# An attention and feed-forward kernel on one core: heads 12 to 15 take the later heads' structure

## The chip, the cores and the metric

The kernel runs on one core of a Trainium2 chip. The metric is the device time of one execution in microseconds, the median of several. The core has TensorE (PE in the profile, with its weight loads as PEld), VectorE (DVE), ScalarE (ACT), GpSimd (POOL) and the queue SP that issues the transfers.

## The reference

Attention over 8 batches of 8 heads, 576 rows and a head dimension of 64, with a mask by blocks of 64 rows, and then a feed-forward layer on the 4608 rows of 512 columns that the heads make together:

```
scores = scale * np.matmul(q, k.transpose(0, 1, 3, 2))
mask = block_i >= block_j                      # blocks of 64
attn = softmax(where(mask, scores, -1e9))      # plus 1e-9 in the sum
x = (attn @ v).transpose(0, 2, 1, 3).reshape(B * S, H * D)
h = x @ w_in                                   # 512 x 2048
out = maximum(0.01 * h, h) @ w_out             # 2048 x 512
```

The weights come as 64-bit floats, and the kernel turns them into pairs of 32-bit parts itself.

## The kernel before

The 64 heads are worked one after the other, two heads making one pair that fills 128 rows of the transposed result. The head's number is `i`, and its batch is `i // 8`. There are two structures of a head, and `PLAIN = 16` (L31) sets where the first ends.

An early head (`i < PLAIN`) loads q and k transposed, scales k (L464), and multiplies in plain 32-bit (L492). The masked rows go through a maximum (L524), an exponential (L533), a reciprocal of the sums (L548, L549) and a scaling (L562 to L564). Then TensorE transposes the probabilities in fifteen blocks (L589), ACT or DVE copies them out of PSUM into `ptf` (L268, L269), and `paired` multiplies them with v for two heads together (L654).

A late head loads q and k in one transfer (`qk_in`, L470), and splits each into a high and a low part in the rounded 32-bit type: `qs` and `ks` (L476 to L483). Its score matmuls run on the parts (L503), its transposes run on VectorE in blocks of 32x32 (`turn`, L677), and four stores to a buffer in device memory and four loads back (`way`, L692, and `ptm`, L699) put the blocks in place. `columns` multiplies with v (L624).

The feed-forward layer runs in 18 chunks of 256 rows. `split_x` splits a chunk's rows into `xh` and `xl` (L739, L740), `ffn1` multiplies with `wih` and `wil` (L755), and `ffn2` with `woh` and `wol` (L782); each chunk has eight steps `u`. A chunk may start once all the heads of its batch are done: chunks 0 and 1 after head 7, chunks 2 and 3 after head 15, and so on. The chunks take turns between `xh0` and `xh1` from chunk 2 on (`side`, L722).

The weights come in 32 pieces (`weight_piece`, L381). A piece is loaded by SP, and built from its integer words on ACT, DVE and POOL (L416 to L440), then split into its two parts. Step `u` of chunk 0 needs the pieces up to number 4u + 4.

The buffers change in three steps. The pools `early` (second row buffers, `ptf`, `vf`, `k_in`, `ident`) and `coded` (the raw words of the weights) are closed when the early heads, and the weights, are done. `second_stage` (L367) puts `qs` and `ks` where `coded` was; `third_stage` (L373) puts `ptm`, `turn`, `vt` and `xh1` where `early` was. A tile in the new pool waits for the tiles whose place it takes.

The order of all instructions is worked out ahead of the launch by `Plan` (L75): a list scheduler with estimated costs, which takes, on each engine, the ready piece of work of the lowest rank. Head `i` has a rank near `i` (first scores `i`, second scores `i + RB`, transposes `i + RT`, values `i + RV`); weight piece n (from 0) has `OFF1 + SL1 * (n + 1) / 32` (L807); step k of the two or three chunks that become ready at head `i` has `i + LEAD + 8k / num` (L833). On the chip every engine works through its list in order.

Of the kernel before, what the change touches and what calls it, by code (L numbers as in the profile page):

```python
# [9 lines left out]
F32 = mybir.dt.float32  # L10
F32R = mybir.dt.float32r
# [6 lines left out]
P = 128  # L18
BLK = 64
D = 64  # L20
S = 576
# [3 lines left out]
CH = 256  # L25
# [2 lines left out]
SIGNS = 5  # L28

WIDE = 512  # L30
PLAIN = 16  # L31
SPREAD = True

RAWS = 3
VALS = 3

RL = -1.611
RP = 20.774
RB = -3.305
RT = 2.986  # L40
RV = -1.976
RX = -2.769
RN = -66.464
RM = -40.088

LEAD = 4.317
LAG = 1.993
RS = -16.364
RG = -5.155
OFF1 = 2.865  # L50
SL1 = 20.541
AHEAD = 0.39

MOVES = {
    "raw": (2200, 675), "k": (900, 1170), "q": (500, 1110), "qk": (1500, 1325), "v": (450, 792),
    "way": (590, 385), "back": (1090, 1095), "out": (690, 354),
}
PADD = 3219.925
HOLD = 72.848
FILL = 235  # L60
FILLTO = -190.328


LOAD = 109
PAD = 463.142
PADO = 31.265
SPARE = 43.439
CHANGE = 100
RATE = 0.449
EDGE = 110  # L70
# [181 lines left out]
def attention_ffn(ctx: ExitStack, tc: tile.TileContext, q2: bass.AP, k2: bass.AP, qk: bass.AP, v: bass.AP, w_in: bass.AP, w_out: bass.AP, out: bass.AP):  # L252
# [3 lines left out]
    ND = DM // P  # L256
# [33 lines left out]
    def fixed(shape, dt, name, n=None, pool=const):  # L290
        if n is None:
            return pool.tile(shape, dt, name=name)
        return [pool.tile(shape, dt, name=f"{name}{i}") for i in range(n)]

    later = {}
# [71 lines left out]
    def second_stage():  # L367
        coded.close()
        pool = ctx.enter_context(tc.tile_pool(name="late", bufs=1, side="right", reuse_waits="tile"))
        later["qs"] = fixed([P, S], F32R, "qs", 2, pool)  # L370
        later["ks"] = fixed([P, 2, S], F32R, "ks", None, pool)

    def third_stage():  # L373
        early.close()
        pool = ctx.enter_context(tc.tile_pool(name="last", bufs=1, reuse_waits="tile"))
        later["ptm"] = fixed([P, turned], F32, "ptm", 2, pool)
        later["turn"] = fixed([P, turned], F32, "turn", 2, pool)
        later["vt"] = fixed([P, NT, D], F32, "vt", 2, pool)
        xh.append(fixed([P, ND, CH], F32R, "xh1", None, pool))

    def weight_piece(num, rank, f, out_side, c0):  # L381
        w, k, kv = WIDE, num % RAWS, num % VALS
# [431 lines left out]
    for i in range(NH + 1):  # L814
        if i == H:
            add([("POOL", 1, narrow)], 0, [], [("h", y) for y in range(2)])
        if i == PLAIN:
            new = [("qs", y) for y in range(2)] + ["kh", "kl"]
            add([("POOL", 1, second_stage)], 0, [y for k in wkeys.values() for y in k], new)
            blocks = ((0, 0), (1, 0), (2, 0), (3, 0), (3, 3), (4, 0), (4, 3), (4, 4))  # L820
            new = [("turn", y, t, j) for y in range(2) for t, j in blocks]
            new += [("ptm", y, b) for y in range(2) for b in range(4)] + [("vt", y) for y in range(2)] + ["qkt"]
            new += [("xh", 1, e) for e in range(0, CH, BLK)]
            old = [("ptf", y, g[0]) for g in tgroups for y in range(2)] + ["ident"]
            old += [(k, y) for k in ("vf", "q", "k") for y in range(2)] + [("p", 1, t) for t in range(1, NT)]
            add([("POOL", 1, third_stage)], 0, [], sorted(set(old), key=str) + new)
        if i in events:
            here = [c for c in range(NCHUNK) if ready[c] == i]
            nxt = events[events.index(i) + 1] if i != events[-1] else i + H
            num = len(here) * NU  # L830
            for k in range(num):
                c, u = here[k // NU], k % NU
                rank = i + LEAD + (nxt - i) * k / num  # L833
                if u == 0:
                    split_x(c, rank - RS)
                ffn1(c, u, rank)
                ffn2(c, u, rank + (nxt - i) * LAG / num + 0.003)
        if i < NH:
            attention(i)
# [37 lines left out]
```

## Time and profile before

| | us |
|---|---|
| median of 3 runs | 1076.86 (1076.47 to 1076.99) |
| the profiled execution | 1080.17 |
| its span, first to last instruction | 1078.4 |
| PE, DVE, ACT, POOL busy | 1053.0, 598.7, 554.3, 237.1 |

The busy times are sums over the whole span. The start, in which weights are built and no chunk is ready, and the end, in which only chunks are left, look different from the middle, so the stretches are read one by one below.

### The profile page before, as it was taken

How to read it: one execution, taken by the hardware profiler on the slowest of the kernel's cores; microseconds unless marked ns; L12 is line 12 of the kernel's file. 1: busy time of each engine (PE TensorE's matmuls, PEld its weight loads, DVE VectorE, ACT ScalarE, POOL GpSimd, SP SyncE). 2: the span in 40 equal slices, each digit the busy share in tenths (PEclk: the TensorE clock that was granted, in tenths of full speed). 3: DMA queues.
4: the chain of work that ended last, by engine and by line, in shares of the span. 5: the costliest groups of instructions: out<-in, count | busy, mean ns of one | idle time of the engine just before them, and what ended most of it. 6: DMA issues, size and time to landing. Idle time of an engine off the chain costs nothing.

```text
span 1078.4 us, 19058 instructions
## 1 busy us (share of the span) xinstructions
PE 1053.0 (98%) x6976; PEld 912.6 (85%) x6976; DVE 598.7 (56%) x1649; ACT 554.3 (51%) x1335; POOL 237.1 (22%) x209
## 2 busy tenths in 40 slices
PE   6889999999999999999999999999999999999998
PEld 4568888988888888888898888898888888999997
DVE  5988882667767677665544567666656660001000
ACT  6998863555545455555544555554555542222222
POOL 3343430221222011112131120212121201221221
PEclk8999999999999999999999999999999999999999
DMA  5555521358777676766454557666676752000000
GB/s 164 167 170 152 171 77 54 111 174 229 219 213 210 187 212 204 197 203 188 140 156 124 172 149 212 194 185 184 181 199 167 212 159 79 2 20 21 1 20 20
DMA packets 89886, 159.07 MB, mean 148 GB/s; under 512 B 9408, under 2 KB 74944, under 8 KB 89792
## 3 DMA queue, kind: packets, MB, share of 16 engines
q1 hardware_dynamic: 89792, 157.85, 50.3%
q8 instruction: 55, 0.90, 0.4%
q14 instruction: 39, 0.32, 0.1%
HBM read 104.33 MB, written 53.48 MB: 146 GB/s over the span
## 4 chain that ended last, share of the span: by engine, by line
PE 86%; DMA 5%; ACT 4%; DVE 3%; issue 1%; SPq 0%; ACTq 0%; DVEq 0%
PE p_h L755 34%; PE p_o L782 33%; PE p_s L503 6%; PE p_t L624 6%; DMA qk_in<-in_qk 3%; PE p_s L492 3%; ACT prow L533 2%; PE p_t L589 1%; PE p_t L654 1%; DVE turn L677 1%; DMA raw<-in_w_out 1%; DVE nmrec L524 1%; DMA raw<-in_w_in 1%; DMA out<-ob 1%; ACT prow L564 0%
## 5 line engine op out<-in xcount | busy, mean ns | idle before, releaser
L755 PE MATMUL p_h<-xh,wih 128*128 128x256 f32 x1152 | 317.7, 281 | 0.4 <-ACT xh L268 0.4
L755 PE MATMUL p_h<-xh,wil 128*128 128x256 f32 x1152 | 314.5, 278 | 0.0
L755 PE MATMUL p_h<-xl,wih 128*128 128x256 f32 x1152 | 299.9, 278 | 0.0
L279 POOL TENSOR_TENSOR gl<-g,gh 128x512 fp32r<-128x512 f32 x115 | 149.5, 1300 | 674.0 <-ACT gh L268 509.5
L755 PEld LDWEIGHTS p_h<-xh,wih 128*128 128x128 f32 x1152 | 216.6, 188 | 12.5 <-issue 2.4
L755 PEld LDWEIGHTS p_h<-xh,wil 128*128 128x128 f32 x1152 | 217.0, 188 | 0.6
L755 PEld LDWEIGHTS p_h<-xl,wih 128*128 128x128 f32 x1152 | 208.1, 188 | 8.2
L533 ACT ACTIVATE prow<-p_s,nmrec 128x448 f32<-128x448 f32 x300 | 154.3, 524 | 91.6 <-DVE nmrec L524 84.6
L770 ACT ACTIVATE g<-p_h 128x512 f32<-128x512 f32 x144 | 85.9, 597 | 221.5 <-PE p_h L755 219.8
L782 PE MATMUL p_o<-woh,gh 128*128 128x512 f32 x576 | 181.2, 396 | 0.0
L782 PE MATMUL p_o<-wol,gh 128*128 128x512 f32 x576 | 179.3, 392 | 0.0
L782 PE MATMUL p_o<-woh,gl 128*128 128x512 f32 x576 | 179.2, 393 | 0.0
L677 DVE STREAM_TRANSPOSE turn<-prow 128x384 f32<-128x384 f32 (+3 forms) x384 | 141.9, 399 | 11.7 <-ACT prow L564 7.8
L782 PEld LDWEIGHTS p_o<-woh,gl 128*128 128x128 f32 x576 | 108.2, 188 | 24.3
L524 DVE TENSOR_REDUCE nmrec<-p_s 128x1 f32<-128x448 f32 x300 | 127.6, 471 | 1.5
L782 PEld LDWEIGHTS p_o<-wol,gh 128*128 128x128 f32 x576 | 108.2, 188 | 23.5
L564 ACT ACTIVATE prow<-prow,nmrec 128x320 f32<-128x320 f32 (+4 forms) x152 | 78.6, 531 | 36.2 <-DVE nmrec L549 36.2
L503 PE MATMUL p_s<-ks,qs 128*128 128x288 f32 (+4 forms) x528 | 92.7, 309 | 3.7 <-ACT prow L533 3.7
L782 PEld LDWEIGHTS p_o<-woh,gh 128*128 128x128 f32 x576 | 89.8, 188 | 3.5 <-issue 1.3
L503 PEld LDWEIGHTS p_s<-ks,qs 128*128 128x128 f32 x528 | 77.9, 189 | 13.5 <-ACT prow L533 5.7
L278 DVE TENSOR_TENSOR xl<-xr,xh 128x1024 fp32r<-128x1024 f32 (+3 forms) x24 | 23.1, 968 | 110.0 <-PE p_h L755 110.0
L268 ACT CAST gh<-g 128x512 fp32r<-128x512 f32 x107 | 66.3, 620 | 18.2 <-PE p_o L782 16.5
(77 smaller groups left out, 990.5 us busy)
## 6 DMA issues: line engine op xcount, KB each, us to landing
way<-turn SPq DMA_DIRECT2D x192, 224.0 KB, 2.4
ptm<-way SPq DMA_DIRECT2D x192, 224.0 KB, 4.4
qk_in<-in_qk SPq DMA_DIRECT2D x48, 576.0 KB, 5.1
out<-ob SPq DMA_DIRECT2D x35, 256.0 KB, 2.1
raw<-in_w_in SPq DMA_DIRECT2D x16, 512.0 KB, 4.5
raw<-in_w_out SPq DMA_DIRECT2D x16, 512.0 KB, 4.2
vt<-in_v SPq DMA_DIRECT2D x48, 160.0 KB, 3.4
vf<-in_v SPq DMA_DIRECT2D x16, 160.0 KB, 2.8
```

Of the source, the lines that this page charges most:

```text
L268: one = lambda: nc.scalar.copy(dst(), src())
L279: ("POOL", pool2(n), lambda: nc.gpsimd.tensor_sub(dst(), one(), two())),
L492: go = lambda ap=ap, cols=cols, k0=k0, k1=k1, first=first, last=last: nc.tensor.matmul(ap, qk_in[:, z, cols], kt()[:, k0:k1], start=first, ...
L503: nc.tensor.matmul(ap, later["qs"][z][:, cols], moving, start=first, stop=last)
L524: [("DVE", dve(kw[t]), lambda t=t, ap=ap, flat=flat: nc.vector.tensor_reduce(nm[z][: qn[t], at_col[t] : at_col[t] + 1], ap[: qn[t]], axis= ...
L533: nc.scalar.activation(o, ap[: qn[t]], AF.Exp, bias=nm[z][: qn[t], at_col[t] : at_col[t] + 1], scale=1.0, accum_out=sums[z][: qn[t], at_co ...
L564: ("ACT", act(kw[t], True) + 108, lambda: nc.scalar.mul(p(), p(), by)),
L624: nc.tensor.matmul(dst, later["vt"][z][:, j], src, start=start, stop=stop)
L677: nc.vector.transpose(dst, src.rearrange("p (s b i) -> p s b i", b=4, i=32))
L755: nc.tensor.matmul(p_h[z][:, i, :], w[:, d, f * P : (f + 1) * P], (xl if x else xh[y])[:, d, :], start=first and k == 0 and (u > 0 or i == ...
L770: add([("ACT", act(512), lambda: nc.scalar.activation(g, p_h[z], AF.Prelu, alpha=0.01))], rank, [("h", z)], ["g"])
L782: nc.tensor.matmul(p_o[m], a[:, i, m * P : (m + 1) * P], w[:, 2 * u + i, :], start=u == 0 and k == 0, stop=u == NU - 1 and k == 5,)
```

## The change

`PLAIN` goes from 16 to 12, so heads 12 to 15 become late heads. The pools that are opened at the switch are arranged anew: `turn` and `xh1` go where the raw words of the weights were, and `qs` and `ks` go where the early heads' buffers were. The scheduler's constants (ranks, paddings) get other values, and so the order of all the work is another.

```diff
--- before.py
+++ after.py
@@ -28,43 +28,43 @@
 SIGNS = 5
 
 WIDE = 512
-PLAIN = 16
+PLAIN = 12
 SPREAD = True
 
 RAWS = 3
 VALS = 3
 
-RL = -1.611
-RP = 20.774
-RB = -3.305
-RT = 2.986
-RV = -1.976
-RX = -2.769
-RN = -66.464
-RM = -40.088
-
-LEAD = 4.317
+RL = 0.905
+RP = 19.537
+RB = -10.801
+RT = 2.852
+RV = -2.105
+RX = -2.406
+RN = -131.149
+RM = -9.122
+
+LEAD = 8.579
 LAG = 1.993
-RS = -16.364
-RG = -5.155
-OFF1 = 2.865
-SL1 = 20.541
-AHEAD = 0.39
+RS = -17.396
+RG = -8.806
+OFF1 = 0.835
+SL1 = 14.148
+AHEAD = 0.478
 
 MOVES = {
     "raw": (2200, 675), "k": (900, 1170), "q": (500, 1110), "qk": (1500, 1325), "v": (450, 792),
     "way": (590, 385), "back": (1090, 1095), "out": (690, 354),
 }
-PADD = 3219.925
-HOLD = 72.848
+PADD = 2834.081
+HOLD = 89.423
 FILL = 235
-FILLTO = -190.328
+FILLTO = -199.142
 
 
 LOAD = 109
-PAD = 463.142
-PADO = 31.265
-SPARE = 43.439
+PAD = 649.305
+PADO = 29.566
+SPARE = 39.535
 CHANGE = 100
 RATE = 0.449
 EDGE = 110
@@ -367,16 +367,16 @@
     def second_stage():
         coded.close()
         pool = ctx.enter_context(tc.tile_pool(name="late", bufs=1, side="right", reuse_waits="tile"))
-        later["qs"] = fixed([P, S], F32R, "qs", 2, pool)
-        later["ks"] = fixed([P, 2, S], F32R, "ks", None, pool)
+        later["turn"] = fixed([P, turned], F32, "turn", 2, pool)
+        xh.append(fixed([P, ND, CH], F32R, "xh1", None, pool))
 
     def third_stage():
         early.close()
         pool = ctx.enter_context(tc.tile_pool(name="last", bufs=1, reuse_waits="tile"))
         later["ptm"] = fixed([P, turned], F32, "ptm", 2, pool)
-        later["turn"] = fixed([P, turned], F32, "turn", 2, pool)
+        later["qs"] = fixed([P, S], F32R, "qs", 2, pool)
+        later["ks"] = fixed([P, 2, S], F32R, "ks", None, pool)
         later["vt"] = fixed([P, NT, D], F32, "vt", 2, pool)
-        xh.append(fixed([P, ND, CH], F32R, "xh1", None, pool))
 
     def weight_piece(num, rank, f, out_side, c0):
         w, k, kv = WIDE, num % RAWS, num % VALS
@@ -815,12 +815,11 @@
         if i == H:
             add([("POOL", 1, narrow)], 0, [], [("h", y) for y in range(2)])
         if i == PLAIN:
-            new = [("qs", y) for y in range(2)] + ["kh", "kl"]
+            blocks = ((0, 0), (1, 0), (2, 0), (3, 0), (3, 3), (4, 0), (4, 3), (4, 4))
+            new = [("turn", y, t, j) for y in range(2) for t, j in blocks] + [("xh", 1, e) for e in range(0, CH, BLK)]
             add([("POOL", 1, second_stage)], 0, [y for k in wkeys.values() for y in k], new)
-            blocks = ((0, 0), (1, 0), (2, 0), (3, 0), (3, 3), (4, 0), (4, 3), (4, 4))
-            new = [("turn", y, t, j) for y in range(2) for t, j in blocks]
-            new += [("ptm", y, b) for y in range(2) for b in range(4)] + [("vt", y) for y in range(2)] + ["qkt"]
-            new += [("xh", 1, e) for e in range(0, CH, BLK)]
+            new = [("qs", y) for y in range(2)] + ["kh", "kl", "qkt"] + [("vt", y) for y in range(2)]
+            new += [("ptm", y, b) for y in range(2) for b in range(4)]
             old = [("ptf", y, g[0]) for g in tgroups for y in range(2)] + ["ident"]
             old += [(k, y) for k in ("vf", "q", "k") for y in range(2)] + [("p", 1, t) for t in range(1, NT)]
             add([("POOL", 1, third_stage)], 0, [], sorted(set(old), key=str) + new)
```

## Rows read from the trace of the kernel before

**Rows 1.** The page: busy time of the engines, and the chain's shares by engine.

```profile
PE 1053.0 (98%) x6976; PEld 912.6 (85%) x6976; DVE 598.7 (56%) x1649; ACT 554.3 (51%) x1335; POOL 237.1 (22%) x209
...
PE 86%; DMA 5%; ACT 4%; DVE 3%; issue 1%; SPq 0%; ACTq 0%; DVEq 0%
```

**Rows 2.** Windows: stretch, length, busy time (instructions) by engine, clock, DMA share, GB/s.

```profile
0.00:78.76 78.76, 61.24 (x321) 42.17 (x321) 62.08 (x170) 65.72 (x176) 30.16 (x49) 0.93 0.55 166
78.76:155.15 76.39, 76.39 (x490) 63.01 (x491) 66.39 (x158) 61.61 (x149) 29.04 (x22) 1.00 0.48 147
155.15:208.50 53.35, 53.35 (x359) 47.44 (x358) 24.64 (x61) 22.65 (x51) 8.04 (x7) 1.00 0.15 50
208.50:330.00 121.50, 120.35 (x824) 105.84 (x823) 85.82 (x246) 67.96 (x170) 29.04 (x22) 1.00 0.74 208
```

**Rows 3.** PE's timeline, heads 7, 9, 10: start, length, line, tiles, matmuls.

```profile
73.69 1.78 PE L654 MATMUL p_t<-ptf,vf 128*64 128x448 f32 x12
...
88.22 1.45 PE L492 MATMUL p_s<-k_in,qk_in 128*128 128x448 f32 x4
89.26 0.86 PE L782 MATMUL p_o<-woh,gh 128*128 128x512 f32 x2
89.96 0.63 PE L782 MATMUL p_o<-wol,gh 128*128 128x512 f32 x2
...
90.89 1.03 PE L589 MATMUL p_t<-ident,prow 128*128 128x128 f32 x8
91.68 0.71 PE L782 MATMUL p_o<-woh,gh 128*128 128x512 f32 x2
...
94.54 1.62 PE L492 MATMUL p_s<-k_in,qk_in 128*128 128x288 f32 x8
96.00 0.93 PE L589 MATMUL p_t<-ident,prow 128*128 128x128 f32 x7
96.69 0.71 PE L782 MATMUL p_o<-woh,gh 128*128 128x512 f32 x2
```

**Rows 4.** PE's timeline, late heads: head 16's first scores, then 17's and 20's.

```profile
193.64 0.86 PE L503 MATMUL p_s<-ks,qs 128*128 128x448 f32 x4
...
211.56 1.03 PE L503 MATMUL p_s<-ks,qs 128*128 128x288 f32 x7
212.42 0.63 PE L782 MATMUL p_o<-woh,gh 128*128 128x512 f32 x2
...
244.60 0.86 PE L503 MATMUL p_s<-ks,qs 128*128 128x448 f32 x4
245.31 0.28 PE L755 MATMUL p_h<-xh,wih 128*128 128x256 f32 x1
```

**Rows 5.** The chain that ended last: values of heads 10/11, 14/15 and 18/19.

```profile
124.03 2.84 PE p_t L654 x20
...
182.47 2.84 PE p_t L654 x20
...
260.90 2.96 PE p_t L624 x28
```

**Rows 6.** Instruction groups of DVE from 62 to 154 us: the building of weights.

```profile
L422 DVE SCALAR_TENSOR_TENSOR val<-raw,val 128x512 int32<-128x512 int32 x23 | 18.6, 810 | 0.0
L427 DVE SCALAR_TENSOR_TENSOR val<-raw,val 128x512 int32<-128x512 int32 x18 | 13.7, 764 | 0.0
L418 DVE TENSOR_SCALAR val<-val 128x512 int32<-128x512 int32 x22 | 9.1, 418 | 1.7 <-ACT val L271 1.7
```

**Rows 7.** The page and the instruction groups: what a late head adds on DVE.

```profile
L677 DVE STREAM_TRANSPOSE turn<-prow 128x384 f32<-128x384 f32 (+3 forms) x384 | 141.9, 399 | 11.7 <-ACT prow L564 7.8
...
L479 DVE SCALAR_TENSOR_TENSOR qs<-qk_in,qs 64x576 fp32r<-64x576 f32 x48 | 38.1, 793 | 25.0 <-ACT qs L271 23.9
```

**Rows 8.** The page's transfers: size, and time from issue to landing.

```profile
way<-turn SPq DMA_DIRECT2D x192, 224.0 KB, 2.4
ptm<-way SPq DMA_DIRECT2D x192, 224.0 KB, 4.4
```

## The prediction

> **What bounds the kernel now.** The page comes first. PE is busy 98% of the span, no other engine over 56%, and the chain that ended last lies on PE for 86% [rows 1]. That is an average, so the windows come next, cut where the work changes [rows 2]. Up to 78.76 us, where chunk 0 starts, PE is idle 17.5 of 78.76 while DVE (62.08) and ACT (65.72) are nearly full: the start is bound by the two of them. From 78.76 to 208.5 PE has no gap at all: chunks 0 and 1 fill whatever the heads leave. What differs inside it is DVE: 66.39 of 76.39 in the first part, in which weights are still built, but 24.64 of 53.35 in the second. After 208.5, with the late heads, PE idles 1.15 of 121.5. So behind the start, time is PE's work plus the gaps in it, and what to read is whether the cover (chunks 0 and 1) lasts until the next chunk is allowed.
>
> **What the change takes from PE.** An early head's first score group holds PE from 88.22 to 89.26, 1.04 us, and the matmul pair behind it comes at a spacing of 0.70 where a pair's usual spacing is 0.46 (the transposes that start at 90.89 wait for three such pairs from 89.26: 0.70, then two of 0.46), so 0.24 more: 1.28. The second group takes 94.54 to 96.00, 1.46; the fifteen transposes 0.79 (90.89 to 91.68) and 0.69 (96.00 to 96.69). Together 4.22 us a head [rows 3]. A late head's groups take 0.71 (244.60 to 245.31) and 0.86 (211.56 to 212.42), 1.57 us, and no transpose on PE [rows 4]. The values of a pair go the other way, from 2.84 to 2.96 us [rows 5]. Four heads in two pairs: 4 x 2.65 - 2 x 0.12 = 10.4 us less work on PE. This lies on the path, since it falls in the stretch without a gap.
>
> **What it adds elsewhere.** Each late head has eight transposes of 0.399 us on DVE, 3.2 us, and a step of 0.79 on `qs` [rows 7]; four heads bring 16 us to DVE, from which the copies out of PSUM, shared between ACT and DVE, take a little back. The cover is DVE's idle time behind 155.15, 28.7 us [rows 2]: I cost it at nothing while that lasts; without the cover it is a rival below. SP gets four `way` and four `ptm` issues a head, and one load for q and k in place of two or three. A `ptm` load can't start before its `way` store has landed, so 2.4 + 4.4 us stand between the last transpose of a head and its values [rows 8]. The DMA share is 0.15 in the stretch where these now fall [rows 2], so I take no contention; they are latency, and count below.
>
> **The switch.** Now `qs` and `ks` of head 12 take the place of `ptf` and `k_in`, so they wait for the values of heads 10 and 11. Before, they lay in the weights' place and waited for no early head. I cost this new wait at nothing by itself: the first late scores came at 193.64, 8.3 us after the end of the values of heads 14 and 15 (182.47 + 2.84) [rows 4, 5], so the old order already ran as if it had that wait. Behind the wait stand the copies on ACT and DVE and, by their order, what is queued after them. `turn` and `xh1` in exchange wait for the last weight, and both are wanted later than `qs`, so the weights may be finished during the switch.
>
> **Does the cover last?** Chunk 2 begins at 208.3, as PE comes free of chunk 1. With 10.4 us less work PE comes free at 197.9. The heads up to 15 must be done by then. At the pace of the old rows: values of heads 10 and 11 end at 126.9 [rows 5], first late scores 8.3 later at 135.2, and the values of the second late pair end 70.2 us after the first late scores (260.90 + 2.96 - 193.64) [rows 4, 5], at 205.4; from the values' end to a chunk's first matmul were 3.3 us (73.69 + 1.78 to 78.76) [rows 3, 2]. That is 208.7, 10.8 us too late, and the whole gain would be a gap. But that pace was not forced. In the old order the chunk's steps had ranks from 12.3 (8 + 4.317) upward by half a rank a step, and the transposes of head 15 rank 18, so chunk 1's steps went first; DVE and ACT were not half busy meanwhile [rows 2]. With LEAD at 8.579 the steps begin at rank 16.6, and head 11's transposes (13.9) and head 12's scores go ahead of all of them. The bounds of the gap that remains are 0 and 10.8; I take 2.5, nearer the lower end, since the row of 155.15 to 208.5 shows more than 28 us of free time on both helpers.
>
> **The start.** Weight pieces get lower ranks (piece 15: 13.1 before, 7.9 now) and go before more of heads 0 to 7. A piece costs DVE about 0.81 + 0.8 x 0.76 + 0.42 = 1.8 us, and only about ten of 32 were built by 62 us [rows 6]. Four pieces pulled forward would delay chunk 0 by up to 7.4 us; if the new order packs DVE better (it idles 16.7 of the first 78.76 [rows 2]) it could also save some 3. I take +1, nearest to no change, as pieces already filled DVE's free time.
>
> **The sum.** -10.4 + 2.5 + 1.0 = -6.9 us, from the profiled execution's 1080.17 (its span of 1078.4 and 1.8 around it) to 1073.3. That execution was 3.3 above the median of 1076.86, so the median goes to 1070.0. About 0.2%, 2.2 us, is what a measurement of this kernel can tell from no change.
>
> **Rivals.**
>
> *The switch eats the gain.* Heads 12 to 15 go at the old pace, chunk 2 starts at 208.7, and the end moves by +0.4: 1077. For it: the chain of one head (load, split, scores, maximum, exponential, transposes, two transfers) has one `ks` and one `qk_in`, and no rank shortens it. Against it: the idle helpers.
>
> *Slower: DVE becomes the bound before chunk 2.* From 62 us DVE has 23 pieces (about 49 us with the splits; 41.4 in the three rows [rows 6]), the rest of heads 8 to 11 (3.5 x 4.5, what the 66.39 of the first stretch leave per head beside the weights), and four late heads at about 9 us (85.82 for nine to ten heads from 208.5 to 330 [rows 2]): 101 us, 8 more for chunks 0 and 1. At the 87% of the stretch with weights that is 125 us, to 187; from a head's last transpose to the chunk another 12 for transfers, values and split: 199. That barely holds. If DVE also idles at the switch, waiting for heads 10 and 11 with the weights already built, 10 to 20 us come on top: chunk 2 at 209 to 219, so +1 to +11, about 1082. The point that decides is chunk 2's first matmul: later than 208.3 is slower. The Trainium skill ("VectorE: DVE Perf Modes", section "Rules for kernel authors") puts a 128x128 transpose on TensorE where PSUM will do, and the section "The three transpose paths" says that VectorE's works in blocks of 32x32 only. By that rule the four heads should have stayed as they are; what it would cost here is this rival. The rows so far bear out the cost on DVE, 3.2 us a head, but also that PE is the fuller engine.
>
> *The gain is whole or more.* No gap, and a start that is no later or 2 to 3 us earlier: 1064 to 1066. For it: the order is worked out with all costs together. Against it: the 10.8 us must vanish entirely.
>
> *The change doesn't act as read.* Ranks order only what is ready, and PE's list is fixed ahead by estimated costs; if the estimates hold the heads back as before, it ends like the first rival, and I count it there.
>
> **How the numbers follow.** The forecast, a gain that is partly given back (1066 to 1074): 0.54. Whole or more: 0.11. The switch eats it (within 0.2%): 0.14. DVE bound, slower: 0.21. So faster 0.65, same 0.14, slower 0.21. Both signs hold much, so the likeliest case's own range, 1066 to 1074, stands beside the full one, 1064 to 1080, which leaves out the far half of the slower case and a little at the low end. The predicted time is the likeliest case's, 1070.0.
>
> **What would show it.** Right: PE busy near 1043; L589 with 180 instead of 240 instructions; chunk 0's first matmul near 80; first late scores between 125 and 131; chunk 2's first matmul between 198 and 204, with PE idle a few us ahead of it. Wrong: PE idle 10 us or more between chunk 1 and chunk 2 with DVE over 85% (the slower rival) or half idle (the first); or chunk 0 later than 85. If all of these hold and the time is still off, new gaps behind 330 us, from the new ranks, would be what I missed.

## The result: slower, and the profile after

The change makes the kernel slower: 1085.21 us (median of 4 runs, 1082.82 to 1087.02) against 1076.66 for the kernel before in the same runs, a ratio of 1.0078 with a 95% interval of 1.0055 to 1.0101. The forecast was 1070.0, with a range up to 1080. The profiled execution took 1084.03, its span is 1082.2, 3.8 more than the 1078.4 of before.

The page of the changed kernel: busy time by engine, the chain's shares, and the three groups of the first feed-forward product.

```profile
PE 1052.8 (97%) x6928; PEld 912.3 (84%) x6928; DVE 561.5 (52%) x1552; ACT 567.8 (52%) x1378; POOL 300.1 (28%) x297
...
PE 86%; DMA 7%; ACT 3%; DVE 1%; issue 1%; SPq 1%; ACTq 0%; DVEq 0%
...
L755 PE MATMUL p_h<-xh,wih 128*128 128x256 f32 x1152 | 319.1, 282 | 0.9 <-ACT xh L268 0.9
L755 PE MATMUL p_h<-xh,wil 128*128 128x256 f32 x1152 | 316.8, 280 | 0.0
L755 PE MATMUL p_h<-xl,wih 128*128 128x256 f32 x1152 | 302.6, 281 | 0.4 <-DVE xl L278 0.4
```

PE is busy 1052.8 us, as before (1053.0, [rows 1]), though its work was to fall by 10. Something on PE itself got longer, and it can only just be seen here: the three L755 groups are no part of the change, and the means of the second and third were 278 ns before. A mean on this page is the duration of one matmul, of which more than half lies beside its neighbours, so 2 ns looks like nothing. What counts here is the distance from one start to the next.

So the profile is read again by that distance. For every row of PE's timeline the time to the start of the next row is put down to its line, less what the row waited; the sums over the whole span, in us. PE idle counts the waits behind its first matmul:

| line | before | after | difference | forecast |
|---|---|---|---|---|
| L492, early scores | 49.71 | 40.53 | -9.2 | -10.0 |
| L589, transposes on PE | 27.84 | 22.63 | -5.2 | -5.9 |
| L503, late scores | 77.55 | 83.67 | +6.1 | +6.3 |
| L654 and L624, values | 93.73 | 96.24 | +2.5 | +0.2 |
| L755, feed-forward, first product | 402.15 | 408.23 | **+6.1** | 0 |
| L782, feed-forward, second product | 402.07 | 401.86 | -0.2 | -1.0 |
| PE idle | 16.88 | 20.79 | **+3.9** | +3.5 |

The 1.0 at L782 is part of the forecast's -10.4: it is the wider spacing (0.24 us a head) of the matmul pair behind an early head's first scores. The attention lines fell by 5.8, not by 9.4; the idle time rose about as the forecast had it, but most of it at another place; and the first product, which the change does not touch, took 6.1 more. Where that comes from is the main question of the experiments.

The windows of the changed kernel, cut at the first matmul of chunks 0, 1 and 2 (columns as in [rows 2]):

```profile
0.00:86.80 86.80, 65.23 (x332) 43.86 (x332) 67.22 (x185) 71.66 (x191) 37.25 (x55) 0.92 0.58 176
86.80:146.70 59.90, 58.08 (x387) 49.39 (x388) 50.63 (x102) 44.17 (x99) 12.64 (x10) 1.00 0.44 144
146.70:211.00 64.30, 63.66 (x418) 55.02 (x416) 39.10 (x114) 37.27 (x96) 22.63 (x22) 1.00 0.63 183
211.00:330.00 119.00, 118.44 (x802) 103.94 (x803) 78.69 (x227) 70.26 (x177) 29.19 (x29) 1.00 0.72 200
```

Against [rows 2]: chunk 0 begins at 86.8 instead of 78.8, chunk 2 at 211.0 instead of 208.3. From chunk 0 to chunk 2 it is 124.2 us against 129.6, so this stretch did get shorter. The 8 us were lost ahead of it, in the start. There the windows of 40 to 60 and 60 to 80 us show a PE with less to do and a lower clock. Before:

```profile
40.00:60.00 20.00, 17.57 (x104) 12.29 (x104) 19.22 (x54) 18.59 (x53) 7.38 (x10) 1.00 0.44 135
60.00:80.00 20.00, 16.85 (x102) 11.91 (x99) 17.64 (x43) 18.45 (x46) 8.40 (x7) 0.91 0.65 189
```

After:

```profile
40.00:60.00 20.00, 15.06 (x79) 10.69 (x78) 15.73 (x44) 16.31 (x45) 6.38 (x7) 0.83 0.59 177
60.00:80.00 20.00, 14.14 (x77) 9.42 (x78) 16.17 (x47) 18.20 (x51) 10.04 (x10) 0.88 0.59 171
```

What PE waited for there stands on SP's timeline of the changed kernel, where raw words of the weights go out ahead of a head's q, and in its chain, where that q ends a wait:

```profile
44.78 0.38 SPq L413 DMA_DIRECT2D raw<-in_w_in  x1
...
46.28 0.37 SPq L413 DMA_DIRECT2D raw<-in_w_out  x1
46.71 0.47 SPq L466 DMA_DIRECT2D qk_in<-in_q  x1
```

```profile
46.71 5.95 DMA qk_in<-in_q
52.66 0.14 issue
52.79 2.90 PE p_w L492 x4
...
76.73 2.92 PE p_s L492 x4
```

This q landed 5.95 us after its issue; the two that were issued at 38.68 and 59.70, with no raw words just ahead of them, took 2.5. PE waits 4.08 us for it, and the four matmuls behind the wait then take 2.90 us, where four such matmuls took 1.45 in [rows 3]: twice as long, at half the clock. The granted clock is 0.62 from 50 to 55 us; between the two levels of 1.2 and 2.4 GHz that is a stretch partly at the lower. At 76.73 it happens again behind a wait of 3.85 us for ACT. So these two waits of PE cost more than their own length. The two stretches (columns as above):

```profile
50.00:55.00 5.00, 2.21 (x4) 1.22 (x5) 3.89 (x12) 4.57 (x13) 1.83 (x2) 0.62 0.83 234
75.00:80.00 5.00, 3.27 (x6) 1.46 (x8) 1.48 (x6) 4.79 (x14) 2.80 (x2) 0.51 0.53 154
```

In the first 90 us PE waits for q twice in the changed kernel, and once before (total us, times, longest). First the changed kernel:

```profile
PE p_s L492 <- DMA qk_in<-in_q: 4.6, 1, 4.6
PE p_w L492 <- DMA qk_in<-in_q: 4.1, 1, 4.1
```

Before:

```profile
PE p_s L492 <- DMA qk_in<-in_q: 4.4, 1, 4.4
```

The switch, on PE's timeline of the changed kernel: values of heads 10/11 (the row shows two of 20 matmuls), the first late scores, values of 12/13 (four of 28) and 14/15, head 17's first scores, chunk 2.

```profile
131.99 0.65 PE L654 MATMUL p_t<-ptf,vf 128*64 128x512 f32 x2
...
144.58 0.86 PE L503 MATMUL p_s<-ks,qs 128*128 128x448 f32 x4
...
184.60 1.08 PE L624 MATMUL p_t<-ptm,vt 128*64 128x512 f32 x4
...
205.42 4.05 PE L624 MATMUL p_t<-ptm,vt 128*64 128x512 f32 x28
209.41 0.96 PE L503 MATMUL p_s<-ks,qs 128*128 128x448 f32 x4
211.02 0.39 PE L755 MATMUL p_h<-xh,wih 128*128 128x256 f32 x1 [0.65 <-ACT xh L268]
```

The values of 10/11 come at 131.99 instead of 124.03 [rows 5], late by what the start lost: 45.2 us behind chunk 0, and 45.3 before. So the new order brought heads 10 and 11 no further forward, and the first late scores come at 144.58, where 125 to 131 had been forecast. But PE has next to no gap at the switch: it waits 0.65 us ahead of chunk 2.

### The profile page after: what moved, and what is told of

Same layout as the page of the kernel before. It is cut to its first block, busy times and chain, and to the rows that moved or that the text cites. A ratio compares the mean times of both kernels' runs of the same rounds, so it can differ in the third digit from the quotient of the medians.

```text
span 1082.2 us, 19120 instructions
## 1 busy us (share of the span) xinstructions
PE 1052.8 (97%) x6928; PEld 912.3 (84%) x6928; DVE 561.5 (52%) x1552; ACT 567.8 (52%) x1378; POOL 300.1 (28%) x297
## 4 chain that ended last, share of the span: by engine, by line
PE 86%; DMA 7%; ACT 3%; DVE 1%; issue 1%; SPq 1%; ACTq 0%; DVEq 0%
PE p_h L755 35%; PE p_o L782 34%; PE p_s L503 7%; PE p_t L624 6%; DMA ptm<-way 1%; DMA qk_in<-in_qk 1%; PE p_s L492 1%; ACT prow L533 1%; DMA way<-turn 1%; DMA k_in<-in_k 1%; DMA raw<-in_w_in 1%; PE p_w L492 1%; PE p_t L654 1%; DMA out<-ob 1%; DMA qk_in<-in_q 1%
## 5 line engine op out<-in xcount | busy, mean ns | idle before, releaser
L755 PE MATMUL p_h<-xh,wih 128*128 128x256 f32 x1152 | 319.1, 282 | 0.9 <-ACT xh L268 0.9
L755 PE MATMUL p_h<-xh,wil 128*128 128x256 f32 x1152 | 316.8, 280 | 0.0
L755 PE MATMUL p_h<-xl,wih 128*128 128x256 f32 x1152 | 302.6, 281 | 0.4 <-DVE xl L278 0.4
L279 POOL TENSOR_TENSOR gl<-g,gh 128x512 fp32r<-128x512 f32 x122 | 159.8, 1310 | 430.3 <-ACT gh L268 311.0
L755 PEld LDWEIGHTS p_h<-xh,wih 128*128 128x128 f32 x1152 | 216.6, 188 | 12.8 <-issue 2.9
L755 PEld LDWEIGHTS p_h<-xh,wil 128*128 128x128 f32 x1152 | 218.1, 189 | 0.5
L755 PEld LDWEIGHTS p_h<-xl,wih 128*128 128x128 f32 x1152 | 207.9, 188 | 8.5 <-DVE xl L278 0.7
L533 ACT ACTIVATE prow<-p_s,nmrec 128x448 f32<-128x448 f32 (+1 forms) x300 | 154.3, 522 | 81.8 <-DVE nmrec L524 68.3
L677 DVE STREAM_TRANSPOSE turn<-prow 128x128 f32<-128x128 f32 (+3 forms) x416 | 154.1, 402 | 67.7 <-ACT prow L564 28.5
L782 PE MATMUL p_o<-woh,gh 128*128 128x512 f32 x576 | 180.9, 395 | 0.0
L782 PE MATMUL p_o<-wol,gh 128*128 128x512 f32 x576 | 180.2, 394 | 0.0
L782 PE MATMUL p_o<-woh,gl 128*128 128x512 f32 x576 | 179.2, 392 | 0.0
L562 POOL TENSOR_SCALAR prow<-prow,nmrec 128x448 f32<-128x448 f32 (+4 forms) x111 | 76.8, 695 | 281.7 <-DVE nmrec L549 224.8
L782 PEld LDWEIGHTS p_o<-woh,gl 128*128 128x128 f32 x576 | 108.2, 188 | 25.3
L782 PEld LDWEIGHTS p_o<-wol,gh 128*128 128x128 f32 x576 | 108.2, 188 | 24.3
L564 ACT ACTIVATE prow<-prow,nmrec 128x320 f32<-128x320 f32 (+4 forms) x183 | 85.2, 493 | 38.9 <-DVE nmrec L549 38.8
L503 PE MATMUL p_s<-ks,qs 128*128 128x288 f32 (+4 forms) x572 | 99.6, 307 | 1.3 <-ACT prow L533 1.2
L503 PEld LDWEIGHTS p_s<-ks,qs 128*128 128x128 f32 x572 | 85.4, 189 | 11.4 <-ACT prow L533 3.0
L782 PEld LDWEIGHTS p_o<-woh,gh 128*128 128x128 f32 x576 | 90.5, 188 | 4.0 <-issue 1.1
```

What stands on the lines that cost most here:

```text
L279: ("POOL", pool2(n), lambda: nc.gpsimd.tensor_sub(dst(), one(), two())),
L503: nc.tensor.matmul(ap, later["qs"][z][:, cols], moving, start=first, stop=last)
L533: nc.scalar.activation(o, ap[: qn[t]], AF.Exp, bias=nm[z][: qn[t], at_col[t] : at_col[t] + 1], scale=1.0, accum_out=sums[z][: qn[t], at_co ...
L562: ("POOL", pool1(kw[t]), lambda: nc.gpsimd.tensor_scalar(p(), p(), by, 1.0, op0=ALU.mult, op1=ALU.mult)),
L564: ("ACT", act(kw[t], True) + 108, lambda: nc.scalar.mul(p(), p(), by)),
L677: nc.vector.transpose(dst, src.rearrange("p (s b i) -> p s b i", b=4, i=32))
```

## The experiments

**How they are compared.** Each table gives the median with the ratio to the kernel before in the same runs, the first matmul of chunks 0 and 2 and PE's idle time behind its first matmul in the profiled execution, and the mean distance from one L755 matmul to the next (neighbouring single matmuls on PE's timeline) in the even chunks from 2 on, which read `xh1`, and in the odd ones from 3 on, which read `xh0`. In the kernel before these are 115.8 and 115.7 ns, in the changed one 119.0 and 117.0. Addresses are bytes in a partition, from the compiled programs. A filler's line moves the line numbers behind it up by one (in `before_xl_shift32` by two).

### The new places, the ranks, and where xh1 lies

The new places put `xh1` at 225248, where before it was at 214080; before, it lay like `xh0` and `xl` 64 past a multiple of 512, now 480 past one, and at no multiple of 64. Four kernels ask whether the first product slows by the new places, and whether the weights' ranks cost the start.

`before_new_places` is the kernel before with the second and third hunk of the change alone (`second_stage`, `third_stage`, and the plan's lists that belong to them).

> The kernel before (PLAIN 16, its constants) with the new places alone. Theory 'place': even chunks go from 115.8 to 119 ns, and with some loss at the switch (qs now waits for the early heads) the time rises by 4 to 7 us, to about 1082. Rival 'constants and order': the places cost nothing, 1077.

`old_weight_ranks` is the changed kernel with three constants put back.

```diff
-OFF1 = 0.835
-SL1 = 14.148
-AHEAD = 0.478
+OFF1 = 2.865
+SL1 = 20.541
+AHEAD = 0.39
```

> The changed kernel with the weights' ranks of before (OFF1, SL1, AHEAD): pieces go behind more of heads 0 to 7. Theory 'weights too early': chunk 0 starts 4 to 8 us earlier than 86.8, near 80, the first late scores move with it from 144.6 to about 138, and the time falls by 4 to 8 us. Rival: the start is bound by DVE and ACT together and the weights are needed by then, so the gap only moves behind chunk 0: time unchanged within 2 us, PE idle between 90 and 140 us.

`xh1_first` is the changed kernel with two lines of `second_stage` exchanged, which puts `xh1` at 210912 (480 past a multiple of 512 again).

```diff
-        later["turn"] = fixed([P, turned], F32, "turn", 2, pool)
         xh.append(fixed([P, ND, CH], F32R, "xh1", None, pool))
+        later["turn"] = fixed([P, turned], F32, "turn", 2, pool)
```

> The changed kernel with xh1 allocated ahead of turn, at 210912, another place that is 32 past a multiple of 64; same order of the work. If the place matters by its offset from a multiple of 64, the even chunks stay at 119 ns and the time at 1085. If it is the neighbourhood of the address (the region of the memory, or what lies beside it), the spacing changes. If it is the order, nothing moves.

`xh1_shift32` is the changed kernel with a filler of 32 bytes behind `xh1`, which moves it down to 225216, a multiple of 64 (448 past a multiple of 512).

```diff
         xh.append(fixed([P, ND, CH], F32R, "xh1", None, pool))
+        fixed([P, 8], F32, "shift", None, pool)
```

> The changed kernel with a tile of 32 bytes put behind xh1, so that xh1 moves from address 225248 (32 past a multiple of 64) to 225216 (a multiple of 64), as its old place 214080 was; the order of the work is the same. Theory 'place': the first feed-forward matmuls are slower because of where xh1 lies. Then the spacing of L755 matmuls in the even chunks falls from 119 to about 116 ns, and the time by 4 to 6 us, to about 1080. Rival 'order': the spacing comes from how the work is interleaved. Then nothing moves: 1085, spacing 119 ns.

| kernel | us, ratio [95%] | chunk 0, 2 | idle | even, odd ns |
|---|---|---|---|---|
| before_new_places | 1083.68, 1.0058 [1.0043, 1.0073] | 77.1, 206.8 | 14.0 | 119.2, 116.7 |
| old_weight_ranks | 1089.26, 1.0114 [1.0096, 1.0133] | 77.7, 213.2 | 23.8 | 119.1, 116.7 |
| xh1_first | 1081.45, 1.0044 [1.0026, 1.0062] | 85.1, 208.0 | 17.9 | 119.0, 116.9 |
| xh1_shift32 | 1079.93, 1.0024 [1.0004, 1.0043] | 88.8, 211.7 | 19.0 | 117.6, 116.4 |

The kernel before with nothing but the new places is slower by 0.58%, although its chunks 0 and 2 begin earlier than before and PE idles less: the loss is in the distance, 119.2 ns. `xh1_first` keeps the distance, as expected, but not the expected time: it took 3.8 us less than the changed kernel, with a start 1.7 us earlier and 2.9 us less idle time, so a few us between two kernels of one order need not come from the distance. Moving `xh1` by 32 bytes, with the same order of work, takes the distance to 117.6, not to the expected 116, and some of the time. With the weights' old ranks chunk 0 begins 9 us earlier, at 77.7, and yet the whole gets slower: from chunk 0 to chunk 2 it then takes 135.5 us instead of 124.2, and 8.1 of them are waits instead of 2.5. So the ranks do set the start, and with these three put back the time is lost behind it.

### Moved back to 64 past a multiple of 512

`shift416` is the changed kernel with a filler of 416 bytes, so that `xh1` lies at 224832, 64 past a multiple of 512 as before. The order of the work is the same; `turn`, which lies ahead of `xh1` in the same pool, moves by 416 bytes too.

```diff
         xh.append(fixed([P, ND, CH], F32R, "xh1", None, pool))
+        fixed([P, 104], F32, "shift", None, pool)
```

> The changed kernel, order unchanged, xh1 moved by 416 bytes to 224832, which has the same remainder by 512 (64) as xh0, xl and the old xh1; the move by 32 bytes had remainder 448. If the remainder by 512 (or 256) sets the rhythm of the first feed-forward matmuls, the even chunks come to 116 ns (117.6 with 32 bytes, 119 without) and the time to about 1078 to 1079. If the region of the memory sets it, it stays at 117.6 and the time at 1080.

`before_new_places_416` is `before_new_places` with this filler.

> The kernel before with the new places and xh1 moved by 416 bytes. The new places alone cost 6 us. If all of that was the address of xh1: 1077 to 1078, even chunks at 116 ns. If the wait of qs on the early heads costs something too: 1080 or more with the spacing back at 116.

`before_shift32` asks the other way round: the kernel before, with its places and its order, and `xh1`, the last tile of its pool, moved alone from 214080 to 214112.

```diff
         later["vt"] = fixed([P, NT, D], F32, "vt", 2, pool)
+        fixed([P, 8], F32, "shift", None, pool)
         xh.append(fixed([P, ND, CH], F32R, "xh1", None, pool))
```

> The kernel before, same order, xh1 moved by 32 bytes to 214112 (remainder 32 by 64). Theory 'offset': even chunks rise from 115.8 to about 119 ns and odd ones by about 1, the time by 5 to 6 us, to 1082. Rival 'region': nothing moves, 1077.

| kernel | us, ratio [95%] | chunk 0, 2 | idle | even, odd ns |
|---|---|---|---|---|
| shift416 | 1077.22, 0.9989 [0.9966, 1.0012] | 85.1, 208.5 | 19.6 | 116.1, 116.4 |
| before_new_places_416 | 1076.85, 1.0008 [0.9987, 1.0030] | 76.5, 206.3 | 13.3 | 116.1, 116.0 |
| before_shift32 | 1082.80, 1.0049 [1.0034, 1.0065] | 76.8, 206.5 | 13.8 | 118.8, 116.0 |

This settles the sign. A filler takes 8.0 us off the changed kernel and 6.8 off the old kernel with the new places, and 32 bytes in the untouched old kernel cost 0.49%. The chain of waits shows it where nothing else runs, in chunk 16 (an even one), when all heads are done: a piece is twelve L755 matmuls, and six of L782 lie between two pieces. The changed kernel:

```profile
988.83 1.42 PE p_h L755 x12
990.25 1.39 PE p_o L782 x6
991.64 1.43 PE p_h L755 x12
994.46 1.43 PE p_h L755 x12
```

`shift416`, where L755 has become L756:

```profile
989.01 1.39 PE p_h L756 x12
990.40 1.37 PE p_o L783 x6
991.77 1.39 PE p_h L756 x12
994.53 1.39 PE p_h L756 x12
```

From piece to piece 2.81 us against 2.76. The six matmuls of L782 take part in it, 1.39 against 1.37, though none of their tiles moved. A chunk has 16 such pieces and eight chunks read `xh1`, which makes an estimate of 8 x 16 x 0.053 = 6.8 us (the changed kernel's thirteen pieces from 988.83 to 1025.40 give 2.813, twelve of `shift416` 2.760). `before_shift32` has both in one execution, chunk 15 on `xh0` and chunk 16 on `xh1`:

```profile
952.49 1.39 PE p_h L756 x12
955.25 1.39 PE p_h L756 x12
...
991.34 1.42 PE p_h L756 x12
994.15 1.42 PE p_h L756 x12
```

The changed kernel does not show this contrast: its chunk 15, which reads `xh0` and `xl` at their old places, has the slow rhythm as well.

```profile
952.36 1.42 PE p_h L755 x12
955.17 1.41 PE p_h L755 x12
```

### What of the address counts

With 64 and 480 past a multiple of 512 fast and slow, and 448, a multiple of 64, in between, it was open what matters. Four more kernels: `before_shift448` (as `before_shift32`, with a filler of 112 words, `xh1` at 214528) and `shift160` (as `shift416`, with 40 words, `xh1` at 225088), each seen once; then two that also move the tiles that are read in turn with `xh1`. `before_all_shift32` puts `xh0`, `xl` and `xh1` 32 bytes further together, `before_xl_shift32` moves `xl` alone of the three by 32. All that lies behind moves too, by 32 bytes in the one and by 256 in the other.

```diff
+    fixed([P, 8], F32, "shift")
     xh = [fixed([P, ND, CH], F32R, "xh0")]
     xl = fixed([P, ND, CH], F32R, "xl")
```

```diff
     xh = [fixed([P, ND, CH], F32R, "xh0")]
+    fixed([P, 8], F32, "shift")
     xl = fixed([P, ND, CH], F32R, "xl")
+    fixed([P, 56], F32, "shift2")
```

> The kernel before with one edit, a filler of 448 bytes per partition ahead of xh1, so that xh1 begins at 214528 (a multiple of 512) and not at 214080 (64 past one). Theory 'the place counts by its remainder to 64': spacing of the FFN1 matmuls 115.7 to 116.1 ns in the even chunks as in the odd ones, time 1076 to 1078. Rival 'the remainder to 512 counts, 64 is good and all else worse': even chunks 117 to 119 ns, 1079 to 1083.

> The kernel after with one edit, a filler of 160 bytes per partition behind xh1, so that xh1 begins at 225088 (320 past a multiple of 512, a multiple of 64). Theory 'remainder to 64': even chunks at 115.8 to 116.3 ns, time 1076 to 1079, as with the filler of 416 bytes. Rival 'remainder to 512': like the filler of 32 bytes (448 past, 117.6 ns) or worse, 1079 to 1082.

> The kernel before with one edit, a filler of 32 bytes per partition ahead of xh0, so that xh0, xl and xh1 all begin 96 past a multiple of 256 and not 64 past one (the early heads' and the later tiles behind them move by 32 as well). Theory 'the place itself counts': FFN1 matmuls at 118 to 120 ns in the even and the odd chunks alike, time 12 us over the kernel before or more, about 1089. Rival 'only the distance between the tiles that are read in turn counts': 115.7 to 116.3 ns in both, 1076 to 1078.

> The kernel before with one edit, a filler of 32 bytes per partition ahead of xl and one of 224 behind it, so that xl alone begins 96 past a multiple of 256, while xh0 and xh1 stay 64 past one. Theory 'the place itself counts': a third of the FFN1 matmuls read xl, so both kinds of chunks slow down by a third to two thirds of the 3 ns that xh1 cost the even chunks, 117 to 118 ns, time 1079 to 1084. Rival 'only the distance counts': xl now lies 32 off from both, so 118 to 120 ns in both kinds of chunks, about 1088.

All places together; `xh0` and `xl` lie 64 past a multiple of 256 in all but the last two:

| kernel | xh1 past a multiple of 256 (of 512) | even, odd ns |
|---|---|---|
| before | 64 (64) | 115.8, 115.7 |
| shift416 | 64 (64) | 116.1, 116.4 |
| shift160 | 64 (320) | 116.2, 116.4 |
| xh1_shift32 | 192 (448) | 117.6, 116.4 |
| before_shift32 | 96 (96) | 118.8, 116.0 |
| changed kernel | 224 (480) | 119.0, 117.0 |
| before_shift448 | 0 (0) | 120.1, 115.8 |
| before_all_shift32 | 96, as xh0 and xl | 118.6, 118.6 |
| before_xl_shift32 | 64, xl at 96 | 118.4, 118.3 |

`before_shift448` took 1086.68 against 1079.96 of the kernel before beside it, `shift160` 1081.34; the last two took 1.0070 [1.0045, 1.0095] and 1.0095 [1.0069, 1.0122] of the kernel before. Neither theory of the first pair held in both runs: a multiple of 64 is not enough, and 320 past a multiple of 512 is as good as 64. Of the places tried, those 64 past a multiple of 256 are fast and the four others (0, 96, 192, 224) slow, each by its own amount. The last pair shows that it is not the distance between these three tiles: moved together, all chunks slow down, by 0.7% where about 12 us had been expected, and `xl` alone, which a third of the matmuls read, is enough to slow all of them, to more than the 117 to 118 ns expected. The weights' tiles lay where they were in all runs, so a distance to them is not excluded. In the chain of `before_xl_shift32` chunk 15 has the slow rhythm, where `before_shift32` had the fast one:

```profile
952.53 1.42 PE p_h L757 x12
955.36 1.42 PE p_h L757 x12
```

Why one place goes with a faster rhythm than another stays open. So does why the odd chunks, whose own tiles did not move, are at 117.0 in the changed kernel and at 116.4 with `xh1` mended, while with the old places they stay at 115.7 to 116.0 where `xh1` alone is moved (116.7 in `before_new_places`). In the changed kernel it is chunks 15 and 17 that differ, when all heads are done: 117.7 ns in both, against 115.4 and 115.5 in `xh1_shift32`; the odd chunks from 3 to 13 are alike within 0.3.

### What the change is worth with xh1 in its place

In this section "ranks" stands for all of the scheduler's constants, old or new. `old_constants_416` is `before_new_places_416` with `PLAIN = 12` and the old ranks, `plain16_new_constants_416` and `plain14_new_constants_416` are `shift416` with another `PLAIN`. In the last pair, both with the filler and the new places, the building of the weights leaves out the step that gives them their signs (L426 to L432: some 25 of DVE's steps, and a few of ACT and POOL), to take work off the helpers: once with `PLAIN = 16` and the old ranks, once with 12 and the new ones.

```diff
-PLAIN = 12
+PLAIN = 16
```

```diff
-            if num % SIGNS:
-                add([("DVE+", dve(w), lambda: nc.vector.scalar_tensor_tensor(
-                    bits(), word(1), -2147483648, bits(), op0=ALU.bitwise_and, op1=ALU.bitwise_or
-                ))], rank, [t_key], [v_key])
...
```

> PLAIN 12 and the new places, xh1 moved by 416 bytes, with all constants of before. If the new constants cost time (chunk 0 at 86.8 for 78.8): chunk 0 near 79, time under the run with the new constants by 3 us or more, about 1072 to 1076. If the new constants are what makes PLAIN 12 work (the weights must be ready earlier): slower, 1083 or more, with PE idle before chunk 2.

> PLAIN 16 with the new constants and new places, xh1 moved by 416 bytes: the fourth corner beside 1076.9 (16, old), 1081.8 (12, old) and 1077.2 (12, new). If the new constants are better only because PLAIN 12 needs early weights, they cost PLAIN 16 some 4 to 8 us (chunk 0 near 85): 1081 to 1085. If they are better by themselves, 1072 to 1076.

> PLAIN 14, otherwise as the changed kernel with xh1 moved by 416 bytes. PE is relieved by half as much (5.2 us) and the weights may be 6 to 8 us later without starving PE, but these constants still build them early. Theory 'start': between the two corners with these constants, 1076 to 1082. A version better than both (under 1075) if the late heads' chain before chunk 2 is what costs.

> PLAIN 16, constants of before, new places, xh1 moved by 416 bytes, and the sign bits of the weights left out (L427 and, for every fifth piece, L431 and L432): 25 x 0.75 us less on DVE, 7 x 0.68 on ACT while weights are built. A measure of how far DVE and ACT bound the first 210 us. Expected: chunk 0 at 70 to 74 us for 76.5, and 2 to 6 us less time than 1076.9.

> The same work left out, with PLAIN 12, the new constants, new places, xh1 moved by 416 bytes (1077.2 with the signs). Theory 'start': PLAIN 12 gives back its 10 us because the weights must be built earlier on full DVE and ACT. With 19 us less on DVE it gets ahead of the same kernel with PLAIN 16 by 4 to 10 us, about 1064 to 1069. Rival 'chain of a late head': chunk 2 waits for heads 12 to 15 at 12 us each whatever the helpers do. Then both fall alike and the difference stays within 2 us.

| PLAIN, ranks, kernel | us, ratio [95%] | chunk 0, 1, 2 | idle |
|---|---|---|---|
| 16, old: before_new_places_416 | 1076.85, 1.0008 [0.9987, 1.0030] | 76.5, 153.2, 206.3 | 13.3 |
| 12, old: old_constants_416 | 1081.84, 1.0049 [1.0030, 1.0068] | 76.4, 152.0, 212.5 | 24.9 |
| 16, new: plain16_new_constants_416 | 1081.01, 1.0034 [1.0021, 1.0047] | 83.6, 152.5, 213.8 | 17.4 |
| 14, new: plain14_new_constants_416 | 1075.36, 0.9980 [0.9963, 0.9996] | 83.6, 148.8, 210.7 | 16.2 |
| 12, new: shift416 | 1077.22, 0.9989 [0.9966, 1.0012] | 85.1, 143.9, 208.5 | 19.6 |
| 16, old, no signs: no_sign_plain16 | 1074.39, 0.9969 [0.9951, 0.9987] | 75.0, 144.3, 204.7 | 11.7 |
| 12, new, no signs: no_sign_plain12 | 1069.34, 0.9921 [0.9897, 0.9945] | 78.4, 146.7, 203.0 | 16.5 |

With the old ranks the four heads lose 5.0 us: chunk 0 is as early as before, but then PE starves between 135 and 150 us, behind ACT's exponentials of the late heads (5.5 us) and behind weights that are late (2.2 us). `old_constants_416` in that window, and what PE waited for from 120 to 165:

```profile
135.00:150.00 15.00, 7.34 (x35) 5.63 (x34) 13.14 (x29) 8.33 (x20) 5.73 (x5) 0.71 0.25 82
```

```profile
PE p_s L504 <- ACT prow L534: 5.5, 2, 4.8
PE p_h L756 <- ACT wih L268: 1.2, 1, 1.2
...
PE p_h L756 <- DVE wil L278: 0.6, 1, 0.6
PE p_h L756 <- POOL wil L279: 0.4, 1, 0.4
```

`shift416` in the same window, with the new ranks:

```profile
135.00:150.00 15.00, 15.00 (x101) 13.81 (x100) 9.51 (x19) 7.25 (x15) 3.45 (x4) 1.00 0.13 41
```

PE is busy 7.34 of 15 us at a clock of 0.71 in the one, all 15 at 1.00 in the other; DVE has 13.14 us of work there against 9.51. The new ranks avoid the hole, and pay for it in the start, where chunk 0 comes 7 to 9 us later (83.6 and 85.1 against 76.5). That it is the earlier weights which avoid it is not shown by itself: `old_weight_ranks`, where they alone are late again, has PE busy all 15.00 us of this window and its waits earlier. With the new ranks held fixed, going from 16 to 12 gains 3.8 us (1081.01 to 1077.22; the intervals of the ratios do not meet), and 14 gains 5.65. With some of the weights' work left out, both are faster, and the four heads with their ranks bring 5.0 us (1074.39 to 1069.34) where they bring nothing with all of it (1076.85 to 1077.22): the change is worth more as the helpers have less to do before chunk 2. Chunk 0 of `no_sign_plain16` came at 75.0, a little later than the 70 to 74 expected. `plain14_new_constants_416` is the best version that computes all: 1075.36, below both kernels, though by little. The theory of the start had expected it between 16 and 12, and its rival, the late heads' chain ahead of chunk 2, under 1075; it fits the rival better, so that this chain costs something too is likely, but not shown. The page of this version: PE is busy 7.3 us less than in the changed kernel.

```profile
PE 1045.5 (98%) x6952; PEld 909.2 (85%) x6952; DVE 554.4 (52%) x1535; ACT 563.7 (53%) x1374; POOL 309.2 (29%) x301
```

## Why the prediction was wrong

**The exchange of places.** The step that failed outright was in "The switch": it asked of `turn`, `xh1`, `qs` and `ks` only what they wait for in their new places, and costed the exchange at nothing. Nobody waits for `xh1`; it was put where the matmuls that read it follow each other at 119.0 ns instead of 115.8. That is +6.1 us in the table by lines, 5.6 of PE's busy time (1047.2 on the page of `shift416`), 6.8 by the rhythm of the pieces and 8.0 in the medians of the changed kernel and `shift416`, a part of which is the start: it is most of the loss of 8.5, and without it the result would have been "within 0.2%" (0.9989). The last sentence of the prediction looked for something missed in new gaps behind 330 us. There were none (1.2 us of waits, where it had been 2.6); the busy time itself had grown.

**PE's work, -10.4.** Right for the matmuls that went: L589 has 180 instead of 240, and L492, L589 and L503 of four heads at the full clock are -10.0, -5.9 and +6.3 by the rows that it named, beside the 1.0 at L782. But -5.8 was measured on the attention lines instead of -9.4, since the heads that stayed got dearer. L492 fell by 9.2 only and L589 by 5.2, 1.5 us lost, most of it where the clock was at half in the start. The values took 2.3 more: about 1.1 in those of the early heads, at the half clock, and 1.1 in one late pair (205.42: 4.05 us instead of 2.96), where the clock was full and the weight loads waited (0.84 us ahead of the one at 206.45). The prediction took durations from a stretch with the full clock, and did not ask whether its own later start would keep it.

**The start, +1.** Mis-sized, and the second step that failed: it measured +8.1. The mechanism was in the text, and so was the size of the move: 20 transfers of raw words are issued ahead of chunk 0 where there had been 16, and four pieces pulled forward were to cost up to 7.4 us. But the value was taken near zero, "as pieces already filled DVE's free time". The pieces did not go into free time: DVE idles 19.6 us ahead of chunk 0, where it had idled 16.7. What the traces show in its place is waits, and the half clock behind them: SP issued raw words ahead of a head's q, and PE waited 8.7 us for q where it had been 4.4, while its waits for ACT's exponentials stayed as they were (11.5 us, before 12.4). By distances, about 3.6 of the 8.1 us are waits, 2.4 matmuls that got dearer, and 1.9 a group of scores and four transposes that lay behind chunk 0 before. `old_weight_ranks` shows that the ranks do it (77.7 with the old ones), and that putting them back costs more than it gains. The helpers' work counts as well: with the signs left out chunk 0 comes at 78.4 instead of 85.1 (`no_sign_plain12` against `shift416`). How the waits divide between the transfers and the helpers stays open. The prediction's own sign of being wrong, "chunk 0 later than 85", came.

**The cover and the switch, +2.5.** Right in the sum: PE waits 2.5 us between chunk 0 and chunk 2 (1.82 and 0.64 in the windows), though only 0.65 of it ahead of chunk 2. The distance from chunk 0 to chunk 2 fell by 5.4, against the 7.9 that the forecast's terms make for it (-10.4 + 2.5), but the stretch holds 192 matmuls of L782 instead of 174: 18 that lay behind chunk 2's first matmul before, some 4.1 us (nine pairs at 0.46). The new wait of `qs` was rightly costed at nothing: 9.8 us from the end of the values of heads 10/11 (131.99 + 2.84) to the first late scores, against 8.3, and `before_new_places_416`, which has this wait with the old order, takes as long as the kernel before. The 16 us that four late heads bring to DVE were nearly right as well: 13.7 at the old ranks (611.3 on the page of `old_constants_416`, 597.6 of `before_new_places_416`) and 15.0 at the new ones (561.6 of `shift416`, 546.6 of `plain16_new_constants_416`). What the prediction did not look at is that the new ranks take 51.0 us off DVE and give POOL 73.0 (546.6 and 310.7 against 597.6 and 237.7, both with `PLAIN = 16`). So DVE was busy 157.0 us up to chunk 2 (67.22 + 50.63 + 39.10), against 153.1 in [rows 2].

**The rivals.** "Slower" named chunk 2 between 209 and 219 and about 1082. Both numbers were met, 211.0 and 1085, by another mechanism: in the last stretch before chunk 2 DVE is busy 39.10 of 64.30 us, so it bounds nothing there. Its mechanism is seen in part in `old_constants_416`, where DVE has 13.14 of 15 us and PE starves. "The switch eats the gain" named 1077 and chunk 2 at 208.7: this is `shift416` (1077.22, 208.5), again for another reason, a start later by 6.3 us (85.1) and not the pace of the late heads (from first late scores to the end of the second late pair 64.9 us, 205.42 + 4.05 - 144.58, where 70.2 had been the old pace). Behind "Slower" stood a rule of the Trainium skill ("VectorE: DVE Perf Modes", "Rules for kernel authors": a 128x128 transpose belongs on TensorE where PSUM will do as its target). No run tests it by itself, as a late head has other score matmuls too; for the four heads as a whole what follows from it holds at the old ranks, +5.0 us, and does not at the new ones, -3.8. So here the order of the work decides, and what the helpers still have to do before chunk 2.

**The range.** 1064 to 1080 held the kernel with the place mended (1077.22) and not the one as changed: an effect of which the trace of before has no row was given no width at all.

## What to carry to other kernels

Where a change moves a tile that matmuls read, compare the distance from start to start of the same matmuls before and after, in a stretch where nothing else runs: three nanoseconds on some 1500 of the matmuls, and what slowed with them, came to 5 to 8 us here, as much as the whole change was to gain, and a filler of some bytes is all that it takes to try another place. A change that takes work off the full engine in the middle of a kernel can be given back in the start, as here; read where the first wait of the new order lies, and at which clock the work behind it runs. And test each part of a bundled change alone: here the four heads with their ranks were worth nothing by themselves (1077.22 against 1076.85), and the exchange of places made the loss.

## What the runs showed of the hardware

The rhythm of matmuls went with where in a partition the tiles lie that they stream. 256 columns of the rounded 32-bit type follow each other at 115.8 to 116.2 ns in chunks that read `xh1` from a place 64 past a multiple of 256 bytes, and at 117.6 to 120.1 from the four other places that were tried (0, 96, 192 and 224 past one). One of the two tiles that are read in turn is enough: with `xl` alone of them moved by 32 bytes all chunks ran at 118.3 to 118.4. But the place of the streamed tile is not the whole of it: the matmuls of L782 slowed with them (six in 1.39 us against 1.37), and so did chunks 15 and 17 of the changed kernel, whose tiles had not moved (117.7). The share of PE stays at 97 to 98% through all of it, and the page's mean of one matmul moves by 1 to 4 ns; PE's busy time shows a loss (1064.4 us with `xl` moved, 1053.0 before), and the distance shows where it is.
